# A state-space convolution and a gated MLP on one core: first transform in full matmuls and one-buffer units, statistics on ScalarE, gate products and adds first in the queues

## The chip, the cores and the metric

The kernel runs on one core of one Trainium2 chip. Its time is device microseconds (us) of that core. A profiled execution gives a "span", about 2 us shorter than the run's time. A run is called "slow" when it is over 1.5% above the fastest of the same kernel, and "fast" otherwise. Medians are over all four runs of a kernel; one run each of full2, b_both, dma125 and best1, and one of the kernel before in every set but the second, were slow. All profiles are of fast runs alone. A ratio is the mean time of one kernel's fast runs over that of the other's fast runs of the same rounds, so it is not quite the ratio of the medians quoted.

Engines: PE is TensorE (matmuls), PEld its weight loads, DVE is VectorE, ACT is ScalarE, SP issues the DMAs.

## The reference, cut to what matters

```python
xn = layernorm(A_q)                        # 2048 tokens x 640
# A: causal convolution over all 2048 tokens, per channel, through an FFT of length 4096
kv = (4-tap shift of k) * v
y  = irfft(rfft(kv) * rfft(ssm_k))[:S] + kv * ssm_D
# B: gated MLP, 640 -> 1728 -> 640
h  = sigmoid(xn @ w_gate) * (xn @ w_up)
out = A_q + xn * y + h @ w_down
```

## The kernel before

There are two streams of work. The **MLP** is dense matmuls. The **convolution** is a long chain: ten sub-blocks, each going through tap products (DVE), first transform (PE), eviction (ACT), second transform (PE), eviction (ACT), complex product (DVE), third transform (PE) and eviction (ACT). After five sub-blocks comes a last transform (16 groups of matmuls) for that half of the channels. Its result goes to DRAM, is loaded again in token order, multiplied and added.

A small list scheduler inside the kernel records all operations and fixes the order on every engine from estimated durations, dependences, buffers and priorities (lower number first). PSUM is split into four one-bank buffers `g` (MLP, transposes, last transform) and two two-bank buffers `c` (first three transforms).

```python
def mm2(i, out, lhs, rhs, start, stop):        # two 64-row halves of the array side by side
    for h in range(2):
        rs = slice(64 * h, 64 * h + 64)
        nc.tensor.matmul(out[h], lhsT=lhs[rs], rhs=rhs[rs], start=start, stop=stop)

def rec_st1(idx, pri, dp):                     # first transform of one sub-block: 2 units
    for jq in range(2):
        cs = [f"c1_{idx}_{jq}_{h}" for h in range(2)]     # takes BOTH two-bank buffers
        def f(...):                                       # 8 pairs of 64-row matmuls, 128 columns
            for x in range(2):
                for j in range(4):
                    mm2(j, [q[:, x, j, :] for q in pt], lhs, Fb, True, True)
        pe(8 * mm(128) + 200, f, ..., alloc=[(c, "c") for c in cs] + ...)
        for h in range(2):
            act(1024, <copy c -> T>)
...
def rec_down(tr):                              # down-projection: two g buffers per 128 tokens
    ...
            dve(320, 1, <acc += g>, r=[(pd[i],)], w=[("acc", q)], pri=gpri(pos[0]))
...
# sigmoid (ACT) and gate product (DVE):   pri=pri - BO     with BO = 10
# norm statistics of every block:         8 bn_stats + 4 bn_aggr on DVE for 4 blocks of 128 tokens
```

Of the kernel before, what the change touches and what calls it, by code (L numbers as in the profile page):

```python
# [25 lines left out]
G = 4  # L26
# [15 lines left out]
def _dft_tables():  # L42
    k1 = np.arange(K1, dtype=np.float64)
    n1 = np.arange(N1, dtype=np.float64)
    n2 = np.arange(N2, dtype=np.float64)
    k2 = np.arange(K2, dtype=np.float64)
    odd = 2.0 * k1 + 1.0
    ang = 2.0 * np.pi * np.outer(n1, odd) / 128.0
    F = np.zeros((2, 2, N1, K1, 2, 2))
    for g in range(2):  # L50
        F[:, g, :, :, 0, g] = np.cos(ang)
        F[:, g, :, :, 1, g] = -np.sin(ang)
    F = F.reshape(P, P)
    th = 2.0 * np.pi * n2[:, None, None] * (odd[None, :, None] + 128.0 * k2[None, None, :]) / 8192.0
    M = np.zeros((2, N2, K1, 3, K2))
    M[:, :, :, 0, :] = np.sin(th)[None]
    M[:, :, :, 1, :] = np.cos(th)[None]
    M[:, :, :, 2, :] = -np.sin(th)[None]
    M = M.reshape(P, K1, 3 * K2)
    ph = 2.0 * np.pi * np.outer(k2, n2) / 64.0  # L60
    A = np.zeros((2, K2, N2, 2))
    A[0, :, :, 0] = np.cos(ph)
    A[0, :, :, 1] = np.sin(ph)
    A[1, :, :, 0] = -np.sin(ph)
    A[1, :, :, 1] = np.cos(ph)
    A = A.reshape(P, P)
    t = 64.0 * n1[None, :] + n2[:, None]
    fi = 2.0 * np.pi * odd[:, None, None] * t[None, :, :] / 8192.0
    B = np.zeros((K1, G, N2, 2, G, N1))
    for g in range(G):  # L70
        B[:, g, :, 0, g, :] = np.cos(fi)
        B[:, g, :, 1, g, :] = -np.sin(fi)
    B = B.reshape(P, N2, 2, P)
    J = np.zeros((P, P))
    E = np.zeros((P, P))
    for m in range(P):
        if m % N1:
            J[m - 1, m] = 1.0
        E[m // N1, m] = 1.0
    return _f16_bits(np.concatenate([F, A, J, E], 1)), _f16_bits(M), _f16_bits(B)  # L80
# [164 lines left out]
def kernel(  # L245
# [44 lines left out]
    Mt = cst.tile([P, K1, 3 * K2], U16, name="Mt")  # L290
    Ct = cst.tile([P, 4, P], U16, name="Ct")
    Mb = Mt.bitcast(F16)
    Cb = Ct.bitcast(F16)
    Fb, Ab, Jb, Eb = (Cb[:, i, :] for i in range(4))
    sT = cst.tile([P, 4, CG], BF16, name="sT")
# [9 lines left out]
        "w": ([P, NC, 512], BF16), "xn": ([P, DM], BF16), "xnT": ([P, NC, 512], BF16), "sig": ([P, 512], BF16),  # L305
        "st": ([P, 4, 18], F32), "kt": ([P, 5360], BF16), "vt": ([P, 5120], BF16),
        "ht": ([P, JS, 2, N2], BF16), "kvt": ([P, 2, N2, JS], BF16),
# [13 lines left out]

    def pe(dur, fn, **kw):
        plan.op("PE", dur * 1e-3, fn, **kw)
# [12 lines left out]

    BO = 10.0
    GA, GB = 10.0, 135.0
    CA, CB = 30.0, 210.0

# [33 lines left out]
    def load_small(pri):  # L374
        dma(lambda: nc.sync.dma_start(Ct[:], Cdram.ap().rearrange("p (c n) -> p c n", c=4)), 128, 1024, w=[("C",)], pri=pri)
        dma(lambda: nc.sync.dma_start(tl["sr"].rearrange("p a b -> p (a b)")[0:G], srow.rearrange("o (g n) -> (o g) n", g=G)), 5, 1280, w=[("sr",)], alloc=[("sr", "yt")], pri=pri)
# [98 lines left out]
    def rec_st1(idx, pri, dp):  # L475
        half, sub = divmod(idx, NSUB)
        hb = f"ht{idx}"
        hr = [(hb, g, p) for g in range(G) for p in range(2)]
        T = f"T{idx}"
        for jq in range(2):  # L480
            cs = [f"c1_{idx}_{jq}_{h}" for h in range(2)]

            def f(jq=jq, cs=cs):
                pt = [tl[c].rearrange("p (x j n) -> p x j n", x=2, j=4) for c in cs]
                for x in range(2):
                    for j in range(4):
                        jj = 4 * jq + j
                        lhs = tl[hb][:, jj] if x else tl[f"kvt{idx}"][:, :, :, jj]
                        lhs = lhs.rearrange("p b n -> p (b n)")
                        mm2(j, [q[:, x, j, :] for q in pt], lhs, Fb, True, True)  # L490
            q = pri + dp * jq / 2
            pe(8 * mm(128) + 200, f, r=[("C",), (f"kvt{idx}",)] + hr + ([(T, "a")] if jq else []),
               w=[(c,) for c in cs] + ([] if jq else [(T, "a")]),
               alloc=[(c, "c") for c in cs] + ([] if jq else [(T, "T")]), pri=q)
            for h in range(2):
                act(1024, lambda jq=jq, h=h, c=cs[h]: nc.scalar.copy(
                    out=tl[T][:, jq, :, :, 2 * h:2 * h + 2],
                    in_=tl[c].rearrange("p (x k g) -> p x k g", x=8, g=2)), r=[(cs[h],)], w=[(T, jq, h)], pri=q)

    def rec_st2(idx, pri, dp):  # L500
        T, S_ = f"T{idx}", f"S{idx}"
        for kb in range(2):
            cs = [f"c2_{idx}_{kb}_{b}" for b in range(2)]

            def f(kb=kb, cs=cs):
# [6 lines left out]
            q = pri + dp * kb / 2  # L512
            pe(32 * mm(64) + 250, f, r=[(T, j, h) for j in range(2) for h in range(2)] + ([(S_, "a")] if kb else []) + [("M", kb)],
               w=[(c,) for c in cs] + ([] if kb else [(S_, "a")]),
# [29 lines left out]
    def rec_st3(idx, pri, dp):  # L544
        half, sub = divmod(idx, NSUB)
        S_ = f"S{idx}"
        for b in range(2):
            c = f"c3_{idx}_{b}"

            def f(b=b, c=c):  # L550
                pa = tl[c].rearrange("p (q j n) -> p q j n", q=2, j=4)
                for q in range(2):
                    for j in range(4):
                        nc.tensor.matmul(pa[:, q, j, :], lhsT=tl[S_][:, 4 * b + 2 * q, j * P:(j + 1) * P], rhs=Ab,
                                         start=True, stop=True)

            def ev(b=b, c=c):
                d0 = 16 * sub + 8 * b
                nc.scalar.copy(out=vview(half).rearrange("p n r d -> p (n r) d")[:, :, d0:d0 + 8],
                               in_=tl[c].rearrange("p (j n) -> p n j", j=8))  # L560
            q = pri + dp * b / 2
            z = sub == 0 and b == 0
            pe(8 * mm(128), f, r=[(S_, "R", 0), (S_, "R", 1), ("C",)], w=[(c,)],
               alloc=[(c, "c")] + ([("V", "V")] if idx == 0 and b == 0 else []), pri=q)
            act(1024, ev, r=[(c,)], w=[("V", (sub + 1 - half) % 6, b)], pri=q)

    def rec_st4(half, pri, dp):
        vr_ = [("V", s + 1 - half, b) for s in range(NSUB) for b in range(2)]
        for q in range(8):
            y = f"yt{half}_{q}"  # L570
            for e in range(2):
# [13 lines left out]
                pq = pri + dp * i4 / 16  # L585
                pe(8 * mm(80), f, r=[(bt,)] + vr_, w=[(c,)], alloc=[(c, "g")], pri=pq)
                act(320, lambda y=y, c=c, e=e: nc.scalar.activation(
# [8 lines left out]
    def rec_ln(tr, pri, spri):  # L596
# [13 lines left out]
        vi = lambda: tl[b].bitcast(I32)[:, :, 15]  # L610
        for i in range(4):
            for s2 in range(2):
# [7 lines left out]
        def rsq():  # L620
            nc.vector.tensor_scalar(ve(), var(), 1e-5, None, op0=ALU.add)
            nc.vector.tensor_scalar(yi(), vi(), 1, None, op0=ALU.logical_shift_right)
# [13 lines left out]
        for i in range(4):  # L636
# [3 lines left out]
            dve(640, 2.2, lambda i=i, x_=x_: nc.vector.tensor_scalar(  # L640
                tl[x_][:], acc[:, 4 * tr + i, :], mv(i)[:, 0:1], tl[b][:, i, 14:15], op0=ALU.subtract, op1=ALU.mult),
                r=[("acc", 4 * tr + i), (b, i, "r"), (b, i, "mv")], w=[(x_,)], alloc=[(x_, "xn")],
# [11 lines left out]
    def rec_fc(tr, n):  # L654
# [5 lines left out]
        for u in range(1 if last else 2):  # L660
# [21 lines left out]
            if last:  # L682
                act(512, lambda c=c: nc.scalar.activation(tl[sg][64:P, :], tl[c][0:64, :], ACT.Sigmoid),
                    r=[(c,)], w=[(sg,)], alloc=[(sg, "sig")], pri=pri - BO)
                dve(512, 1, lambda c=c: nc.vector.tensor_tensor(hT[64:P, fc, :], tl[sg][64:P, :], tl[c][64:P, :],
                                                                ALU.mult),
                    r=[(c,), (sg,)], w=[(hk, fc)], pri=pri - BO)
            elif u == 0:
                act(512, lambda c=c: nc.scalar.activation(tl[sg][:], tl[c][:], ACT.Sigmoid),
                    r=[(c,)], w=[(sg,)], alloc=[(sg, "sig")], pri=pri - BO)  # L690
            else:
                dve(512, 1, lambda c=c: nc.vector.tensor_tensor(hT[:, fc, :], tl[sg][:], tl[c][:], ALU.mult),  # L692
                    r=[(c,), (sg,)], w=[(hk, fc)], pri=pri - BO)

    def rec_down(tr):
        hT = hTs[tr % 2]
        hk = f"hT{tr % 2}"
        for t4 in range(4):
# [18 lines left out]
            for i in range(2):  # L717
                dve(320, 1, lambda i=i, q=q, pd=pd: nc.vector.tensor_tensor(
                    acc[:, q, 320 * i:320 * i + 320], tl[pd[i]][:, 0:320], acc[:, q, 320 * i:320 * i + 320], ALU.add),
                    r=[(pd[i],)], w=[("acc", q)], pri=gpri(pos[0]))  # L720

# [3 lines left out]
    def rec_xhat(pri):  # L725
# [6 lines left out]
        for q in range(NQ):  # L732
            st = f"st{q // 4}"
            dve(640, 2.2, lambda q=q, st=st: nc.vector.tensor_scalar(
                xqv(q), xqv(q), tl[st][:, q % 4, 12:13], tl[st][:, q % 4, 14:15], op0=ALU.subtract, op1=ALU.mult),
                r=[(st, q % 4, "r"), (st, q % 4, "mv")], w=[(f"xq{q // 8}", q)], pri=pri - 3)
# [151 lines left out]
```

## Time and profile before

| | us |
|---|---|
| median run (timed with the changed kernel) | 285.7 |
| span of the profile | 281.4 |
| PE busy / PE idle | 255.8 / 25.6 |
| DVE busy, ACT busy | 206.3, 154.6 |

The page of the kernel before: engine totals, then PE's busy tenths and granted clock (tenths of full speed) in 40 equal slices.

```profile
span 281.4 us, 7503 instructions
...
PE 255.8 (91%) x3176; PEld 157.4 (56%) x3176; DVE 206.3 (73%) x356; ACT 154.6 (55%) x215; POOL 0.7 (0%) x6
...
PE   7989999998997946999999897999999999999980
...
PEclk9999999999999975999999998999999999999996
```

PE is the fullest engine. The two low clock digits (7 and 5) are at 98 to 113 us. The windows view of the same kernel gives length, busy time and count per engine, then granted clock, DMA share and GB/s:

```profile
80.00:120.00 40.00, 31.53 (x515) 23.69 (x513) 38.19 (x65) 27.31 (x34) 0.00 (x0) 0.87 0.59 69
220.00:260.00 40.00, 38.76 (x413) 25.51 (x412) 23.55 (x43) 16.49 (x30) 0.00 (x0) 1.00 0.61 159
260.00:281.40 21.40, 13.60 (x101) 9.58 (x98) 10.07 (x24) 0.00 (x0) 0.00 (x0) 0.87 0.76 192
```

There are two holes: 8.5 us of PE idle from 80 to 120 us at a lowered clock, and the end. The timeline view shows the first hole's cause. Columns are start, length, engine, line, operation, output and inputs, and in brackets the idle time before it and what ended it.

```profile
97.37 0.30 PE L705 MATMUL g_1436<-wd,hT_80 128*128 128x320 bf16 x1
...
108.55 0.48 DVE L718 TENSOR_TENSOR acc<-g_1317,acc 128x320 bf16<-128x320 f32 x1
...
109.08 0.69 PE L646 MATMUL g_1713<-ident,xn_1529 128*128 128x128 bf16 x5 [2.10 <-DVE acc L718]
...
111.04 0.48 DVE L718 TENSOR_TENSOR acc<-g_1318,acc 128x320 bf16<-128x320 f32 x1
...
112.61 0.48 DVE L718 TENSOR_TENSOR acc<-g_1435,acc 128x320 bf16<-128x320 f32 x1
```

The granted clock (third number from the end) was 0.50 from 101.8 to 112.0 us:

```profile
101.80:112.04 10.24, 6.96 (x155) 6.26 (x155) 9.62 (x13) 6.11 (x8) 0.00 (x0) 0.50 0.18 27
```

PE finished the first two down-projection results (`g_1317`, `g_1318`) at about 92.7 us and the next two at 97.7. DVE began to add them 15 to 18 us later. All four `g` buffers were held until then, so no MLP matmul could run.

### The profile page before, as it was taken

Reading aid. Unit: us, or ns where it says so; the run is one execution under the profiler, and the core shown is the slowest. Engines: PE = TensorE matmul, PEld = TensorE weight load, DVE = VectorE, ACT = ScalarE, POOL = GpSimd, SP = SyncE. Lnnn points to the kernel's source line nnn. Section 1 sums busy time; section 2 is a strip of 40 time slices with the busy share of each in tenths; the row PEclk is TensorE's granted clock in tenths of the full one; section 3 lists DMA queues with packets and bytes.
Section 4 is the critical chain, followed back from the end, with each engine's and each line's share of the span. In section 5 each row is a group of like instructions: output and inputs, shape, how many; then the busy total and the mean of one; then the engine's idle time right before and its main releaser. Section 6 shows DMA issues by size and latency. Waiting matters only on the chain.

```text
span 281.4 us, 7503 instructions
## 1 busy us (share of the span) xinstructions
PE 255.8 (91%) x3176; PEld 157.4 (56%) x3176; DVE 206.3 (73%) x356; ACT 154.6 (55%) x215; POOL 0.7 (0%) x6
## 2 busy tenths in 40 slices
PE   7989999998997946999999897999999999999980
PEld 2844344554545746776775655555545555677760
DVE  7862998899999998998949783057197899412382
ACT  2652324666585485975558876677667646222000
POOL 0000000000000000000000000000000000000000
PEclk9999999999999975999999998999999999999996
DMA  7999886976397920071231576541449357754687
GB/s 203 268 150 146 211 272 141 350 190 168 50 153 104 141 31 13 12 190 45 40 95 21 152 204 227 172 132 48 159 123 341 78 95 182 210 185 170 113 199 273
DMA packets 106993, 42.62 MB, mean 151 GB/s; under 512 B 77196, under 2 KB 102608, under 8 KB 106960
## 3 DMA queue, kind: packets, MB, share of 16 engines
q1 hardware_dynamic: 106960, 42.14, 64.5%
q8 instruction: 25, 0.41, 0.6%
q14 instruction: 8, 0.07, 0.1%
HBM read 36.89 MB, written 5.24 MB: 150 GB/s over the span
## 4 chain that ended last, share of the span: by engine, by line
PE 43%; DMA 9%; DVE 7%; issue 2%; SPq 1%; ACT 0%; DVEq 0%; ACTq 0%
DMA B_2908<-dftB 2%; DMA B_4171<-dftB 2%; DMA B_2729<-dftB 2%; DMA yd<-yt_4298 2%; SPq L437 1%; DMA ht_1899<-in_A_ssm_k_dram 1%; PE g_4389 L705 1%; PE g_2142 L705 1%; PE g_2202 L705 1%; PE g_2288 L705 1%; PE g_2398 L705 1%; PE g_4516 L705 1%; PE g_4471 L705 1%; PE g_4431 L705 1%; PE g_4470 L705 1%
## 5 line engine op out<-in xcount | busy, mean ns | idle before, releaser
L705 PEld LDWEIGHTS <-hT_81 128*128 128x128 bf16 x224 | 21.4, 98 | 9.0 <-issue 0.7
L473 PEld LDWEIGHTS <-Mt 64*128 64x128 f16 x1280 | 21.8, 97 | 7.9 <-issue 7.6
L705 PEld LDWEIGHTS <-hT_80 128*128 128x128 bf16 x224 | 21.0, 98 | 8.7 <-issue 1.1
L779 PE MATMUL c_88<-sig_85,ident 128*128 128x512 bf16 x26 | 8.4, 477 | 1.7 <-POOL ident masks.py:199 1.4
L666 PEld LDWEIGHTS <-w_435 128*128 128x128 bf16 x40 | 3.8, 98 | 5.8 <-DMA w_435<-in_B_w_gate_dram 0.9
L666 PEld LDWEIGHTS <-w_806 128*128 128x128 bf16 x40 | 3.7, 98 | 5.2 <-DMA w_806<-in_B_w_gate_dram 1.0
L666 PEld LDWEIGHTS <-w_562 128*128 128x128 bf16 x40 | 3.8, 98 | 4.4
L666 PEld LDWEIGHTS <-w_2301 128*128 128x128 bf16 x40 | 3.8, 104 | 4.4 <-issue 1.1
L666 PEld LDWEIGHTS <-w_487 128*128 128x128 bf16 x40 | 3.8, 98 | 4.4
L666 PEld LDWEIGHTS <-w_3610 128*128 128x128 bf16 x40 | 3.8, 98 | 4.3
L779 PEld LDWEIGHTS <-ident 128*128 128x128 bf16 x26 | 2.8, 116 | 5.8 <-issue 3.3
L666 PEld LDWEIGHTS <-w_121 128*128 128x128 bf16 x40 | 3.8, 98 | 4.0
L666 PEld LDWEIGHTS <-w_2876 128*128 128x128 bf16 x40 | 3.7, 98 | 4.2
L666 PEld LDWEIGHTS <-w_3171 128*128 128x128 bf16 x40 | 3.7, 98 | 4.1
L666 PEld LDWEIGHTS <-w_3371 128*128 128x128 bf16 x40 | 3.6, 98 | 4.0
L692 DVE TENSOR_TENSOR hT_80<-sig_3039,g_3022 128x512 bf16<-128x512 bf16 x1 | 0.7, 689 | 7.0 <-PE g_3022 L666 7.0
L666 PEld LDWEIGHTS <-w_2067 128*128 128x128 bf16 x40 | 3.6, 98 | 3.8
L666 PEld LDWEIGHTS <-w_932 128*128 128x128 bf16 x30 | 2.8, 97 | 3.4 <-issue 0.4
L676 PEld LDWEIGHTS <-w_98 128*128 128x128 bf16 x80 | 4.6, 98 | 0.0
L613 DVE BATCH_NORM_STATS2 st_105<-acc 128x6 f32<-128x320 bf16 x8 | 3.6, 467 | 1.2 <-DMA acc<-in_A_q_dram 1.2
L531 DVE TENSOR_TENSOR Sb_3277<-S_3053 64x2048 bf16<-64x2048 bf16 x2 | 2.4, 1220 | 2.7 <-ACT S_3053 L517 2.7
L666 PEld LDWEIGHTS <-w_3814 128*128 128x128 bf16 x30 | 2.8, 98 | 2.8
(867 smaller groups left out, 805.0 us busy)
## 6 DMA issues: line engine op xcount, KB each, us to landing
out_dram<-acc SPq DMA_DIRECT2D x8, 320.0 KB, 3.5
acc<-in_A_q_dram SPq DMA_DIRECT2D x3, 640.0 KB, 6.6
Mt<-dftM SPq DMA_DIRECT2D x2, 768.0 KB, 6.3
wd<-in_B_w_down_dram SPq DMA_DIRECT2D x3, 480.0 KB, 4.8
kt_139<-in_A_k_dram SPq DMA_DIRECT2D x4, 320.0 KB, 7.4
vt_190<-in_A_v_dram SPq DMA_DIRECT2D x4, 320.0 KB, 7.1
kt_1114<-in_A_k_dram SPq DMA_DIRECT2D x4, 320.0 KB, 8.2
vt_1329<-in_A_v_dram SPq DMA_DIRECT2D x4, 320.0 KB, 7.6
```

The lines of the kernel that those rows point to most:

```text
L437: dma(lambda g=g, p=p, c0=c0: nc.sync.dma_start(tl[b][g * N1:(g + 1) * N1, :, p, :], h3[:, c0:c0 + JS, :]), 5.5 * JS, 128, w=[(b, g, p)], ...
L473: nc.tensor.matmul(out[h], lhsT=lhs[rs], rhs=rhs[rs], start=start, stop=stop)
L531: dve(2 * JS * P, 2, lambda o=hv[h], i=hv[1 - h]: nc.vector.tensor_tensor(tl[Sb][o], xh(0)[o], xh(1)[i], ALU.mult), r=sk, w=[(Sb, h)], all ...
L613: dve(320, 1, lambda i=i, s2=s2: nc.vector.bn_stats(stat(i, s2), acc[:, 4 * tr + i, s2 * 320:(s2 + 1) * 320]), r=[("acc", 4 * tr + i)], w= ...
L666: nc.tensor.matmul(tl[c][:], lhsT=tl[wb][:, k, o:o + P], rhs=tl[X][:, k, :], start=(k == 0), stop=(k == NC - 1))
L676: nc.tensor.matmul(tl[c][:, ts], lhsT=tl[wb][:, k, o:o + P], rhs=tl[X][:, k, ts], start=(k == 0), stop=(k == NC - 1))
L692: dve(512, 1, lambda c=c: nc.vector.tensor_tensor(hT[:, fc, :], tl[sg][:], tl[c][:], ALU.mult), r=[(c,), (sg,)], w=[(hk, fc)], pri=pri - BO)
L705: nc.tensor.matmul(tl[pd[i]][:, 0:320], lhsT=hT[:, fc, t4 * P:(t4 + 1) * P], rhs=wd[:, fc, 320 * i:320 * i + 320], start=(fc == 0), stop=( ...
L779: plan.op("PE", 0.43 if i < 13 else 0.22, lambda: nc.tensor.matmul(tl["wps"][:, 0:512], lhsT=ident[:], rhs=tl["warm"][:], start=True, stop ...
```

## The change

The intent: evict the first transform one buffer at a time, with each matmul filling the whole array; take work off DVE in its full stretch; and free PSUM sooner by placing gate products and adds ahead of everything else on ACT and DVE. Two further edits come with it: convolution matmuls first on PE (`FST`), and four numbers (`GA, GB, CA, CB`) that spread the convolution among the MLP work.

```diff
-    F = np.zeros((2, 2, N1, K1, 2, 2))          # table 128 x 128, two channel groups per half
+    F = np.zeros((G, N1, K1, 2, G))             # table 128 x 256, four groups at once
 def rec_st1:
-        for jq in range(2):
-            cs = [f"c1_{idx}_{jq}_{h}" for h in range(2)]
-                        mm2(j, [q[:, x, j, :] for q in pt], lhs, Fb, True, True)
-            pe(8 * mm(128) + 200, f, ..., alloc=[(c, "c") for c in cs] + ...)
+        for u in range(4):
+            jq, x = divmod(u, 2)
+            c = f"c1_{idx}_{u}"                  # ONE two-bank buffer
+                    nc.tensor.matmul(pt[:, j, :], lhsT=..., rhs=Fb, start=True, stop=True)   # x4
+            pe(4 * mm(256), f, first=FST, ..., alloc=[(c, "c")] + ...)
 ... (first=FST on the other transforms too; FST = 1000.0, subtracted from the priority)
 def rec_ln:
+        for i in range(4 if tr >= 2 else 0):     # blocks 8 to 15: two ACT passes each
+            Copy(scale=-1/640, accum_out=-mean); Square(bias=-mean, accum_out=sum)
-        for i in range(4):
+        for i in range(4 if tr < 2 else 0):      # bn_stats on DVE
 sigmoids and gate products:
-                    pri=pri - BO
+                    pri=-1.0
 down-projection adds:
-                    pri=gpri(pos[0])
+                    pri=-1.0
-    GA, GB = 10.0, 135.0
-    CA, CB = 30.0, 210.0
+    GA, GB = 20.0, 140.0
+    CA, CB = 35.0, 200.0
```

More of the change, by code (lines that the diff above doesn't have):

```diff
@@ L48, in _dft_tables @@
     ang = 2.0 * np.pi * np.outer(n1, odd) / 128.0
-    F = np.zeros((2, 2, N1, K1, 2, 2))
-    for g in range(2):
-        F[:, g, :, :, 0, g] = np.cos(ang)
-        F[:, g, :, :, 1, g] = -np.sin(ang)
-    F = F.reshape(P, P)
+    F = np.zeros((G, N1, K1, 2, G))
+    for g in range(G):
+        F[g, :, :, 0, g] = np.cos(ang)
+        F[g, :, :, 1, g] = -np.sin(ang)
+    F = F.reshape(P, 2 * P)
     th = 2.0 * np.pi * n2[:, None, None] * (odd[None, :, None] + 128.0 * k2[None, None, :]) / 8192.0
@@ L290 @@
     Mt = cst.tile([P, K1, 3 * K2], U16, name="Mt")
-    Ct = cst.tile([P, 4, P], U16, name="Ct")
+    Ct = cst.tile([P, 5 * P], U16, name="Ct")
     Mb = Mt.bitcast(F16)
     Cb = Ct.bitcast(F16)
-    Fb, Ab, Jb, Eb = (Cb[:, i, :] for i in range(4))
+    Fb, Ab, Jb, Eb = Cb[:, 0:2 * P], Cb[:, 2 * P:3 * P], Cb[:, 3 * P:4 * P], Cb[:, 4 * P:5 * P]
     sT = cst.tile([P, 4, CG], BF16, name="sT")
@@ L305 @@
         "w": ([P, NC, 512], BF16), "xn": ([P, DM], BF16), "xnT": ([P, NC, 512], BF16), "sig": ([P, 512], BF16),
-        "st": ([P, 4, 18], F32), "kt": ([P, 5360], BF16), "vt": ([P, 5120], BF16),
+        "st": ([P, 4, 17], F32), "kt": ([P, 5360], BF16), "vt": ([P, 5120], BF16),
         "ht": ([P, JS, 2, N2], BF16), "kvt": ([P, 2, N2, JS], BF16),
@@ L320, in make, with pe @@
         return pool.tile(shape, dt, name=f"{tag}{i}", tag=f"{tag}{i}")
-    def pe(dur, fn, **kw):
+    FST = 1000.0
+    def pe(dur, fn, first=0.0, **kw):
+        kw["pri"] -= first
         plan.op("PE", dur * 1e-3, fn, **kw)
@@ L335, in mm @@
         return n / 2.4 + 3.0
-    BO = 10.0
-    GA, GB = 10.0, 135.0
-    CA, CB = 30.0, 210.0
+    GA, GB = 20.0, 140.0
+    CA, CB = 35.0, 200.0
     def gpri(p):
@@ L374, in load_small @@
     def load_small(pri):
-        dma(lambda: nc.sync.dma_start(Ct[:], Cdram.ap().rearrange("p (c n) -> p c n", c=4)), 128, 1024, w=[("C",)], pri=pri)
+        dma(lambda: nc.sync.dma_start(Ct[:], Cdram.ap()), 160, 1280, w=[("C",)], pri=pri)
         dma(lambda: nc.sync.dma_start(tl["sr"].rearrange("p a b -> p (a b)")[0:G], srow.rearrange("o (g n) -> (o g) n", g=G)), 5, 1280, w=[("sr",)], alloc=[("sr", "yt")], pri=pri)
@@ L479, in rec_st1, with f @@
         T = f"T{idx}"
-        for jq in range(2):
-            cs = [f"c1_{idx}_{jq}_{h}" for h in range(2)]
-            def f(jq=jq, cs=cs):
-                pt = [tl[c].rearrange("p (x j n) -> p x j n", x=2, j=4) for c in cs]
-                for x in range(2):
-                    for j in range(4):
-                        jj = 4 * jq + j
-                        lhs = tl[hb][:, jj] if x else tl[f"kvt{idx}"][:, :, :, jj]
-                        lhs = lhs.rearrange("p b n -> p (b n)")
-                        mm2(j, [q[:, x, j, :] for q in pt], lhs, Fb, True, True)
-            q = pri + dp * jq / 2
-            pe(8 * mm(128) + 200, f, r=[("C",), (f"kvt{idx}",)] + hr + ([(T, "a")] if jq else []),
-               w=[(c,) for c in cs] + ([] if jq else [(T, "a")]),
-               alloc=[(c, "c") for c in cs] + ([] if jq else [(T, "T")]), pri=q)
-            for h in range(2):
-                act(1024, lambda jq=jq, h=h, c=cs[h]: nc.scalar.copy(
-                    out=tl[T][:, jq, :, :, 2 * h:2 * h + 2],
-                    in_=tl[c].rearrange("p (x k g) -> p x k g", x=8, g=2)), r=[(cs[h],)], w=[(T, jq, h)], pri=q)
+        for u in range(4):
+            jq, x = divmod(u, 2)
+            c = f"c1_{idx}_{u}"
+            def f(jq=jq, x=x, c=c):
+                pt = tl[c].rearrange("p (j n) -> p j n", j=4)
+                for j in range(4):
+                    jj = 4 * jq + j
+                    lhs = tl[hb][:, jj] if x else tl[f"kvt{idx}"][:, :, :, jj]
+                    nc.tensor.matmul(pt[:, j, :], lhsT=lhs.rearrange("p b n -> p (b n)"), rhs=Fb, start=True, stop=True)
+            q = pri + dp * u / 4
+            pe(4 * mm(256), f, first=FST, r=[("C",)] + (hr if x else [(f"kvt{idx}",)]) + ([(T, "a")] if u else []),
+               w=[(c,)] + ([] if u else [(T, "a")]), alloc=[(c, "c")] + ([] if u else [(T, "T")]), pri=q)
+            act(1024, lambda jq=jq, x=x, c=c: nc.scalar.copy(
+                out=tl[T][:, jq, 4 * x:4 * x + 4].rearrange("p j k g -> p (j k g)"), in_=tl[c][:]),
+                r=[(c,)], w=[(T, u)], pri=q)
     def rec_st2(idx, pri, dp):
@@ L512, in rec_st2 @@
             q = pri + dp * kb / 2
-            pe(32 * mm(64) + 250, f, r=[(T, j, h) for j in range(2) for h in range(2)] + ([(S_, "a")] if kb else []) + [("M", kb)],
+            pe(32 * mm(64) + 250, f, first=FST, r=[(T, u) for u in range(4)] + ([(S_, "a")] if kb else []) + [("M", kb)],
                w=[(c,) for c in cs] + ([] if kb else [(S_, "a")]),
@@ L562, in rec_st3 @@
             z = sub == 0 and b == 0
-            pe(8 * mm(128), f, r=[(S_, "R", 0), (S_, "R", 1), ("C",)], w=[(c,)],
+            pe(8 * mm(128), f, first=FST, r=[(S_, "R", 0), (S_, "R", 1), ("C",)], w=[(c,)],
                alloc=[(c, "c")] + ([("V", "V")] if idx == 0 and b == 0 else []), pri=q)
@@ L585, in rec_st4 @@
                 pq = pri + dp * i4 / 16
-                pe(8 * mm(80), f, r=[(bt,)] + vr_, w=[(c,)], alloc=[(c, "g")], pri=pq)
+                pe(8 * mm(80), f, first=FST, r=[(bt,)] + vr_, w=[(c,)], alloc=[(c, "g")], pri=pq)
                 act(320, lambda y=y, c=c, e=e: nc.scalar.activation(
@@ L610, in rec_ln, with f1, f2 @@
         vi = lambda: tl[b].bitcast(I32)[:, :, 15]
-        for i in range(4):
+        for i in range(4 if tr >= 2 else 0):
+            x_ = f"xs{tr}_{i}"
+            ac = ("acc", 4 * tr + i)
+            def f1(i=i, x_=x_):
+                nc.scalar.activation(tl[x_][:], acc[:, 4 * tr + i, :], ACT.Copy, scale=-1.0 / DM, accum_out=tl[b][:, i, 12:13])
+            def f2(i=i, x_=x_):
+                nc.scalar.activation(tl[x_][:], acc[:, 4 * tr + i, :], ACT.Square, bias=tl[b][:, i, 12:13],
+                                     accum_out=tl[b][:, i, 13:14])
+            act(640, f1, r=[ac], w=[(x_,), (b, i, "nm")], alloc=[(x_, "xn")] + ([(b, "st")] if i == 0 else []), pri=spri)
+            act(640, f2, r=[ac, (b, i, "nm")], w=[(x_,), (b, i, "mv")], pri=spri)
+        for i in range(4 if tr < 2 else 0):
             for s2 in range(2):
@@ L620, in rsq @@
         def rsq():
-            nc.vector.tensor_scalar(ve(), var(), 1e-5, None, op0=ALU.add)
+            nc.vector.tensor_scalar(ve(), var(), 1.0 / DM if tr >= 2 else 1.0, 1e-5, op0=ALU.mult, op1=ALU.add)
             nc.vector.tensor_scalar(yi(), vi(), 1, None, op0=ALU.logical_shift_right)
@@ L640, in rec_ln @@
             dve(640, 2.2, lambda i=i, x_=x_: nc.vector.tensor_scalar(
-                tl[x_][:], acc[:, 4 * tr + i, :], mv(i)[:, 0:1], tl[b][:, i, 14:15], op0=ALU.subtract, op1=ALU.mult),
+                tl[x_][:], acc[:, 4 * tr + i, :], mv(i)[:, 0:1], tl[b][:, i, 14:15],
+                op0=ALU.add if tr >= 2 else ALU.subtract, op1=ALU.mult),
                 r=[("acc", 4 * tr + i), (b, i, "r"), (b, i, "mv")], w=[(x_,)], alloc=[(x_, "xn")],
@@ L683, in rec_fc @@
                 act(512, lambda c=c: nc.scalar.activation(tl[sg][64:P, :], tl[c][0:64, :], ACT.Sigmoid),
-                    r=[(c,)], w=[(sg,)], alloc=[(sg, "sig")], pri=pri - BO)
+                    r=[(c,)], w=[(sg,)], alloc=[(sg, "sig")], pri=-1.0)
                 dve(512, 1, lambda c=c: nc.vector.tensor_tensor(hT[64:P, fc, :], tl[sg][64:P, :], tl[c][64:P, :],
                                                                 ALU.mult),
-                    r=[(c,), (sg,)], w=[(hk, fc)], pri=pri - BO)
+                    r=[(c,), (sg,)], w=[(hk, fc)], pri=-1.0)
             elif u == 0:
                 act(512, lambda c=c: nc.scalar.activation(tl[sg][:], tl[c][:], ACT.Sigmoid),
-                    r=[(c,)], w=[(sg,)], alloc=[(sg, "sig")], pri=pri - BO)
+                    r=[(c,)], w=[(sg,)], alloc=[(sg, "sig")], pri=-1.0)
             else:
                 dve(512, 1, lambda c=c: nc.vector.tensor_tensor(hT[:, fc, :], tl[sg][:], tl[c][:], ALU.mult),
-                    r=[(c,), (sg,)], w=[(hk, fc)], pri=pri - BO)
+                    r=[(c,), (sg,)], w=[(hk, fc)], pri=-1.0)
     def rec_down(tr):
@@ L719, in rec_down @@
                     acc[:, q, 320 * i:320 * i + 320], tl[pd[i]][:, 0:320], acc[:, q, 320 * i:320 * i + 320], ALU.add),
-                    r=[(pd[i],)], w=[("acc", q)], pri=gpri(pos[0]))
+                    r=[(pd[i],)], w=[("acc", q)], pri=-1.0)
     def xqv(q):
@@ L734, in rec_xhat @@
             dve(640, 2.2, lambda q=q, st=st: nc.vector.tensor_scalar(
-                xqv(q), xqv(q), tl[st][:, q % 4, 12:13], tl[st][:, q % 4, 14:15], op0=ALU.subtract, op1=ALU.mult),
+                xqv(q), xqv(q), tl[st][:, q % 4, 12:13], tl[st][:, q % 4, 14:15],
+                op0=ALU.add if q >= 8 else ALU.subtract, op1=ALU.mult),
                 r=[(st, q % 4, "r"), (st, q % 4, "mv")], w=[(f"xq{q // 8}", q)], pri=pri - 3)
```

## The prediction

> **What bounds it now.** TensorE: the page gives PE 255.8 of 281.4 us busy, DVE 206.3, ACT 154.6. By windows, though, DVE is the second limit from 40 to 140 us: 93.4 of 100 us busy. In 80-100 and 100-120 us it is busy 16.64 and 14.89 of 20, at a granted clock of 0.74 in the second.
>
> The timeline shows why. The first down-projection groups end on PE at about 92.5 us, but their adds into acc (g_1317, g_1318, g_1435, g_1436) run on DVE only at 108.55-113.4 us, behind norm statistics, taps and products. They hold all four one-bank PSUM buffers ("g"), so no filler matmul can start. Waits of PE between 97 and 114 us: 1.15, 0.70, 1.09, 0.18, 0.70, 2.10, 0.66, together 6.6 us. The idle also halves the clock (skill, "TensorE: Matmul & The Clock Gate", on re-throttling; here matmuls of the second transform take 238 ns instead of 188, and the slices show 7 and 5). My estimate of the clock's cost, from blocks that take 2.7 and 1.9 us instead of 1.0, is 4 us. The stall costs about 11 us.
>
> **What changes.**
> - Adds and gate products first on DVE: buffers come free about 0.5-2 us after PE ends. Removes most of the 11 us, and the wait of 1.58 us at 88 us.
> - Statistics of blocks 8-15: 16 bn_stats (0.46 us) and 8 aggregates (0.19) leave DVE, about 8-9 us of the saturated stretch. ACT gains 16 passes over 640 columns, about 0.7 us each (as the 128x640 copies), 11 us; ACT was busy 60-75% there, so it fits.
> - First transform: a pair-packed unit of 16 half matmuls costs 0.62 us from its start to the next matmul (chain: 187.64 to 188.26), against 8 x 54 ns streaming. The rest is mode switch (skill, "TensorEngine Tiling (Array Packing)", Key Properties: changing mode drains TensorE; this trace agrees). Full matmuls of 256 columns: 8 x 109 ns (half of the 512-column spacing, 216 ns) = 0.87 us. So PE pays 0.25 x 20 = **5 us more**. In return eviction (1.01 us) and matmul can alternate.
> - Tail: after the last down matmul, DVE now does two adds and one final add instead of six operations: about -1 us.
>
> **Sum, on the critical path.** 281.4 + 5 (PE work) - 10 (stall and clock) - 2 (gate-product waits and DVE-late spots) - 1 (tail) = 273.4 us of span; runs read about 2 us longer. The waits for the last transform's tables at 158-173 us (2.5 us idle, clock 0.91) stay: same three buffers and queue. Predicted **275 us**, 268.5 to 282; faster 0.80, same 0.17, slower 0.03.
>
> **What would show each step.**
> - PE stays at about 252-256 us busy (5 more work, 4 less clock), its share rises to 93% or more.
> - No slice between 80 and 125 us below 9 for PE; clock 1.0 there; adds into acc within 2 us of their matmuls.
> - First-transform matmuls 256 columns, about 109 ns apart, 160 of them; 0.87 us per two units.
> - DVE about 198 us, ACT about 165 us.
> - No PE wait over 1 us on adds or gate products; table waits remain.
>
> **What would make it wrong.** ACT's statistics passes in front of evictions of the first and second transform, so that conv-first matmuls wait at PE's head. The conv's chain (evict, product, taps) still too slow, so that filler runs out elsewhere. Worse collisions of table loads with weight loads. Then 280-285. If the freed DVE removes nearly all idle before 225 us, 268.

(In its first paragraph the 16.64 and 14.89 of 20 us are PE's busy time, not DVE's.)

## More of the kernel before

The cost of a paired first-transform unit can be read from the timeline too. Five MLP matmuls take 1.08 us from start to start (65.83 to 66.91):

```profile
66.91 1.24 PE L666 MATMUL g_953<-xnT_131,w_806 128*128 128x512 bf16 x5
68.08 0.28 PE L473 MATMUL c_973<-Ct,kvt_550 64*128 64x128 f16 x1
...
68.70 0.61 PE L666 MATMUL g_954<-xnT_131,w_806 128*128 128x512 bf16 x2
```

From 66.91 + 1.08 = 67.99 to 68.70 is 0.71 us for eight pairs, of which about 0.45 is streaming (0.056 us a pair).

Chips differ between sets of runs, and each set carries its own runs of the kernel before.

## The result, and the profile after

The changed kernel takes 272.6 us (272.1 to 272.9, four runs) against 285.7 us. The ratio is 0.958, interval 0.949 to 0.966. That is 13.1 us by the medians and 10.6 us by the spans (the profile of the kernel before is of a 283.3 us run).

The page of the changed kernel:

```profile
span 270.8 us, 7185 instructions
...
PE 254.7 (94%) x3016; PEld 160.1 (59%) x3016; DVE 199.4 (74%) x332; ACT 166.2 (61%) x247; POOL 0.7 (0%) x6
...
PE   7989799989989899999999989999999999999993
...
PEclk9999999999999999999999999999999999999998
```

Its windows:

```profile
80.00:120.00 40.00, 38.11 (x581) 27.53 (x580) 35.68 (x57) 35.76 (x53) 0.00 (x0) 1.00 0.67 103
220.00:260.00 40.00, 39.20 (x355) 26.41 (x353) 19.13 (x43) 10.02 (x22) 0.00 (x0) 1.00 0.73 188
260.00:270.80 10.80, 6.09 (x45) 4.16 (x43) 2.88 (x7) 0.00 (x0) 0.00 (x0) 0.90 0.45 157
```

PE's busy time is nearly the same (255.8 to 254.7). What fell is its idle time, 25.6 to 16.1 us: 6.6 us of that between 80 and 120 us, and 3.1 us in the tail after the last matmul (273.6 to 281.4 before, 266.1 to 270.8 now). Busy time alone hides part of this, since the same matmuls are also busy for longer at a lowered clock.

The first two adds now start 0.3 and 1.7 us after their last matmul (timeline of the changed kernel):

```profile
95.44 0.30 PE L717 MATMUL g_1191<-wd,hT_80 128*128 128x320 bf16 x1
...
95.88 0.49 DVE L730 TENSOR_TENSOR acc<-g_1190,acc 128x320 bf16<-128x320 f32 x1
...
97.42 0.48 DVE L730 TENSOR_TENSOR acc<-g_1191,acc 128x320 bf16<-128x320 f32 x1
```

The other adds of the first half (1024 tokens) wait up to 3.5 us.

Two of the new first-transform units, with the MLP matmul that follows:

```profile
61.54 0.60 PE L491 MATMUL c_851<-Ct,kvt_555 128*128 128x256 f16 x4
...
61.98 0.60 PE L491 MATMUL c_859<-Ct,ht_507 128*128 128x256 f16 x4
...
62.42 1.24 PE L678 MATMUL g_865<-xnT_131,w_753 128*128 128x512 bf16 x5
```

Two units take 0.88 us where one paired unit of the same work took 0.71. The change makes PE do 20 x 0.17 = 3.4 us more, not less.

A new cost shows at 20 to 60 us, where PE is busy 36.9 us instead of 39.4: it waits for loads (the first line below). From the waits of PE in the changed kernel (waited for: total, times, longest):

```profile
PE g_425 L424 <- DMA kt_140<-in_A_k_dram: 1.6, 1, 1.6
...
PE c_1433 L491 <- ACT T_1411 L495: 1.1, 1, 1.1
PE g_2704 L581 <- DMA B_2608<-dftB: 0.9, 1, 0.9
```

### The profile page after: what moved, and what is told of

It reads as the page before. It is cut to its first block, busy times and chain, and to the rows that moved or that the text cites. A ratio compares the mean times of both kernels' runs of the same rounds, so it can differ in the third digit from the quotient of the medians.

```text
span 270.8 us, 7185 instructions
## 1 busy us (share of the span) xinstructions
PE 254.7 (94%) x3016; PEld 160.1 (59%) x3016; DVE 199.4 (74%) x332; ACT 166.2 (61%) x247; POOL 0.7 (0%) x6
## 4 chain that ended last, share of the span: by engine, by line
PE 53%; SPq 14%; DVE 11%; DMA 11%; ACT 5%; issue 3%; DVEq 0%; ACTq 0%
SPq L439 4%; SPq L421 4%; SPq L419 3%; DMA w_627<-in_B_w_up_dram 3%; DMA yd<-yt_2751 2%; DMA B_4087<-dftB 2%; DMA B_3848<-dftB 1%; DVE acc L730 1%; DMA B_2608<-dftB 1%; DMA w_436<-in_B_w_gate_dram 1%; ACT S_924 L516 1%; DMA w_1787<-in_B_w_gate_dram 1%; DVE Sb_1765 L530 1%; DVE t_1727 L461 1%; PE g_2117 L717 1%
## 5 line engine op out<-in xcount | busy, mean ns | idle before, releaser
L717 PEld LDWEIGHTS <-hT_80 128*128 128x128 bf16 x224 | 21.2, 98 | 7.6
L475 PEld LDWEIGHTS <-Mt 64*128 64x128 f16 x1280 | 20.2, 93 | 6.8 <-issue 6.5
L530 DVE TENSOR_TENSOR Sb_3405<-S_3218 64x2048 bf16<-64x2048 bf16 x2 | 2.4, 1222 | 2.3 <-ACT S_3218 L516 2.2
L530 DVE TENSOR_TENSOR Sb_1425<-S_1244 64x2048 bf16<-64x2048 bf16 x2 | 2.4, 1221 | 2.2 <-ACT S_1244 L516 2.1
```

Source lines behind the costliest of these rows:

```text
L530: dve(2 * JS * P, 2, lambda o=hv[h], i=hv[1 - h]: nc.vector.tensor_tensor(tl[Sb][o], xh(0)[o], xh(1)[i], ALU.mult), r=sk, w=[(Sb, h)], all ...
L717: nc.tensor.matmul(tl[pd[i]][:, 0:320], lhsT=hT[:, fc, t4 * P:(t4 + 1) * P], rhs=wd[:, fc, 320 * i:320 * i + 320], start=(fc == 0), stop=( ...
```

## The experiments

Theory A, that of the prediction: the late adds were the main loss, so the queue places are the main gain, and the first transform costs PE time for little return. Rivals: B, the first transform's one-buffer units are the gain; C, the statistics leaving DVE are the gain. From the second set on there is a Theory D, formed from the first set.

For each run, the table also gives three readings: PE busy between 80 and 120 us with the granted clock; the mean period of the convolution's sub-blocks (start of the second transform of the tenth minus that of the first, over 9); and the end of the last transform's last matmul group ("conv end"), with what is left of the span after it. The last matmul groups of the last transform in the kernel before and in the changed one:

```profile
259.02 0.45 PE L582 MATMUL g_4399<-V_1294,B_4360 128*128 128x80 bf16 x8
243.90 0.45 PE L581 MATMUL g_4175<-V_1180,B_4127 128*128 128x80 bf16 x8
```

| kernel | median us | ratio to before | PE busy 80-120, clock | period | conv end | span minus conv end |
|---|---|---|---|---|---|---|
| before | 284.3 to 285.7 by set | 1 | 31.5, 0.87 | 18.0 | 259.5 | 21.9 |
| changed | 272.6 | 0.958 | 38.1, 1.00 | 16.4 | 244.4 | 26.4 |
| u_adds | 277.4 | 0.975 | 34.5, 1.00 | 16.2 | 242.9 | 32.9 |
| u_st1 | 291.0 | 1.022 | 37.8, 1.00 | 18.2 | 265.7 | 22.6 |
| u_stats | 272.0 | 0.955 | 37.9, 0.96 | 16.3 | 241.8 | 26.4 |
| u_gates | 279.6 | 0.985 | 36.0, 0.96 | 16.5 | 245.2 | 32.1 |
| pairs1 | 272.3 | 0.954 | 37.8, 0.96 | 16.5 | 244.7 | 26.4 |
| full2 | 294.2 | 1.034 | 37.1, 1.00 | 18.8 | 270.3 | 21.2 |
| b_queue | 291.4 | 1.021 | 37.6, 1.00 | 18.3 | 265.8 | 23.5 |
| b_units | 284.3 | 0.996 | 31.7, 0.91 | 17.1 | 251.0 | 31.6 |
| b_both | 273.8 | 0.963 | 35.1, 1.00 | 16.0 | 241.8 | 29.1 |
| u_knots | 280.8 | 0.988 | 34.5, 0.96 | 16.0 | 245.4 | 34.0 |
| dma125 | 274.1 | 0.963 | 39.1, 1.00 | 16.8 | 247.5 | 22.6 |
| best1 | 271.8 | 0.957 | 38.6, 1.00 | 16.7 | 245.2 | 22.6 |

All gave correct results; each has four runs, timed over three rounds.

### First set: one part undone at a time

**u_adds**, the adds back to their late place:

```diff
-   r=[(pd[i],)], w=[("acc", q)], pri=-1.0)
+   r=[(pd[i],)], w=[("acc", q)], pri=gpri(pos[0]))
```

> The changed kernel with one thing undone: the adds of the down-projection go back to their late place in the VectorE queue. Theory A (the gain is the early release of the four one-bank buffers by the adds): the stall near 100-115 us comes back, adds start more than 5 us after their matmuls, the clock falls there, 279 us or more. Theory B (the gain is the first transform's single two-bank units): 273 to 275 us. Theory C (the gain is the statistics leaving VectorE): 273 to 275 us.

277.4 us, so 4.8 us of the gain needs this line. PE is idle for 5.5 of the 40 us from 80 to 120, 3.6 more than in the changed kernel. The clock stayed at 1.00, so the stall is only partly back. That is less than A asked for, and more than B and C.

**u_st1**, the whole first transform as before, with the old table; `first=FST` kept:

```diff
-   for u in range(4):   4 x matmul(256 columns),   alloc=[(c, "c")]
+   for jq in range(2):  8 x mm2(pair, 128 columns), alloc=[(c, "c") for c in cs], first=FST
```

> The changed kernel with the first transform put back to pairs of half matmuls that take both two-bank buffers (everything else kept). Theory B: the waits for both buffers come back, 280 us or more. Theory A: PE work falls by 5 us (0.25 x 20 units), busy PE near 250 us, and the time falls or stays, 268 to 273 us. Theory C: as A.

291.0 us: slower than the kernel before. A had expected 268 to 273, so A falls. PE busy did fall (250.9 us), as A had it, but the time rose by 18 us. The early hole is still filled; the loss is at the end. Windows of u_st1, then its longest wait of PE:

```profile
220.00:260.00 40.00, 31.52 (x411) 23.03 (x411) 18.73 (x33) 14.69 (x23) 0.00 (x0) 0.91 0.51 128
260.00:288.30 28.30, 12.25 (x114) 8.91 (x112) 9.93 (x24) 1.64 (x4) 0.00 (x0) 0.80 0.66 175
```

```profile
PE g L584 <- DVE acc L733: 6.6, 1, 6.6
```

That wait is not where the convolution falls behind: the third transform of its tenth sub-block, before the wait, already ends at 236.2 us, against 217.9 in the changed kernel.

**u_stats**, statistics of all blocks on DVE again:

```diff
-   for i in range(4 if tr >= 2 else 0):   # ACT passes
-   for i in range(4 if tr < 2 else 0):    # bn_stats
+   for i in range(4):                     # bn_stats
```

> The changed kernel with the statistics of blocks 8 to 15 back on VectorE as bn_stats. VectorE gains about 8 us and ScalarE loses about 12. Theory C (the gain is mostly this relief): 279 us or more. Theory A: VectorE is full only from 100 to 140 us (39 of 40), so part of the 8 us shows, 274 to 277 us.

272.0 us (270.0 to 273.1), not to be told from the changed kernel. C falls, and so does A's 274 to 277. DVE is 6.4 us busier, ACT 11.1 us less, and the time does not care.

**u_gates**, sigmoids and gate products back to their old priority:

```diff
-   pri=-1.0        # sigmoid, gate product
+   pri=pri - 10.0
```

> The changed kernel with the sigmoids and gate products back at their old priority (ten below that of their matmul). Every theory: a little slower, 273 to 276 us, since the buffers of gate and up matmuls come free later behind taps and products; if gate products were the main part of the gain, 279 us or more.

279.6 us, slower by 7.0. That is above the 273 to 276 of every theory and inside the branch "279 us or more": next to the rest of the change, the places of the gate products are worth more than those of the adds (4.8).

B had u_st1 right and u_adds wrong. After this set, **Theory D**: the program has two ends, and both must be early. PE must not run out of buffers (late adds and gate products), and the convolution's chain must end early enough. After its last transform there are still the store, the loads, products and adds: 22.6 us in u_st1 (and 21 to 24 in full2 and b_queue below), of which PE has work for only the first few. Freeing the MLP's buffers alone lets the MLP run ahead of the convolution. One-buffer units shorten the chain.

The traces of the three slowest kernels agree. Their last gate or up matmul ends at 220.5 (b_queue), 222.2 (full2) and 223.6 us (u_st1), 13 to 18 us before the third transform of the tenth sub-block does (235.8, 240.4, 236.2). In the changed kernel it ends at 233.0, 15 us after that transform (217.9), so the MLP still has work to fill in.

### Second set: the form and the buffering apart, and each part alone

**pairs1**, one-buffer units kept, in the same order on every engine, but with paired half matmuls:

```diff
-   for j in range(4): nc.tensor.matmul(pt[:, j, :], lhsT=lhs, rhs=Fb)        # 256 columns
+   for j in range(4): mm2(j, [q[:, j, :] for q in pt], lhs, Fb, True, True)  # one half per bank
```

> The changed kernel with the same units of one two-bank buffer each and the same order on every engine, but the matmuls of a unit are again pairs of 64-row halves (one half per bank). Theory D (what the first transform's change is worth is the unit of one buffer, which shortens the convolution's chain; the form of the matmul is not): within 1 us of the changed kernel's 272.6 us, since a unit of four pairs should cost 4 x 55 ns plus about 0.2 us of mode switch, 0.42 us, against 0.44 us for four full matmuls. Rival E (the full matmul itself is the gain, by doing away with the mode switches): 278 us or more.

272.3 us, as D had it. With one-buffer units the form of the matmul costs and brings nothing: in its timeline, a unit of four pairs takes 0.43 us from the end of the MLP matmuls before it (179.37 + 1.08 = 180.45) to the next one (180.88), and a full unit takes 0.44.

```profile
179.37 1.25 PE L680 MATMUL g<-xnT,w 128*128 128x512 bf16 x5
180.55 0.40 PE L475 MATMUL c<-Ct,ht 64*128 64x128 f16 x8
180.88 1.25 PE L680 MATMUL g<-xnT,w 128*128 128x512 bf16 x5
```

**full2**, full matmuls but two buffers per unit:

```diff
-   for u in range(4):   alloc=[(c, "c")]
+   for jq in range(2):  alloc=[(c, "c") for c in cs]     # 8 full matmuls, then two evictions
```

> The changed kernel with the full 256-column matmuls, but in units that take both two-bank buffers at once as before. Theory D: as slow as the kernel with the whole first transform undone (291.0 us) or slower by up to 5 us, since PE has 5 us more to do: 289 to 296 us, with the convolution's last matmul near 265 us. Rival E: 273 to 276 us.

294.2 us (one run, 297.7, was slow), and the conv end is 270.3 where D said "near 265". So the unit of one buffer, with the order that the scheduler plans from it, is the whole value of this part. Against u_st1 (291.0, of another set), which differs by the form of the matmul, full matmuls cost 3.2 us by the medians and 1.3% by the ratios, close to the 3.4 us read above.

**b_queue**, the kernel before with only the queue places:

```diff
-   pri=pri - BO            # sigmoid, gate product
-   pri=gpri(pos[0])        # down-projection adds
+   pri=-1.0                # all three
```

> The kernel before with only the queue places of the change: sigmoids, gate products and down-projection adds first. Theory A as predicted (this is the main gain, 10 to 12 us): 273 to 277 us. Theory D: the stall at 97-114 us goes, but the convolution's chain is as long as before, so the other matmuls run out ahead of it and PE starves at the end: 283 to 292 us, with idle after 220 us in place of that at 100 us.

291.4 us: 5.9 us *slower* than before (ratio 1.021, interval 1.014 to 1.028). This is the prediction's main gain on its own. The early hole is gone (37.6 of 40 busy, clock 1.00), and everything is lost at the end. Windows of b_queue, then its longest waits of PE:

```profile
220.00:260.00 40.00, 30.03 (x402) 22.17 (x400) 21.89 (x43) 14.29 (x23) 0.00 (x0) 0.87 0.51 128
260.00:289.30 29.30, 12.34 (x115) 8.97 (x112) 10.02 (x24) 1.64 (x4) 0.00 (x0) 0.79 0.63 168
```

```profile
PE g L582 <- DVE acc L718: 6.4, 1, 6.4
PE c L554 <- DVE S L537: 3.5, 1, 3.5
```

Its last down-projection matmul ends at 272.3 us, 17 us before the span does. The convolution ends at 265.8, 6.3 us later than before. Part of that is there before the last transform: the third transform of the tenth sub-block ends at 235.8, against 232.2. That gate products and adds now go ahead of the convolution's own work on DVE would explain this part; it was not isolated. The rest comes with the 6.4 us wait. This wait, at 236 to 242 us, is a last-transform group that waits for a `g` buffer: four down results stand in them until 241.6 us, while DVE works through final products and adds that stood ahead of theirs. A wait of 6.6 us at this place is in u_st1 and full2 too, and in neither the kernel before nor the changed one. No run takes it away, so how slow b_queue would be without it is open.

**b_units**, the kernel before with only the new first transform (and its table):

```diff
-   for jq in range(2):  8 x mm2(pair, 128 columns), alloc=[(c, "c") for c in cs]
+   for u in range(4):   4 x matmul(256 columns),   alloc=[(c, "c")]
```

> The kernel before with only the first transform of the change: full matmuls, units of one two-bank buffer. Theory A: late adds still hold the one-bank buffers, 284 to 290 us. Theory D: the chain shortens (last matmul of the last transform before 250 us instead of 259), the stall near 100 us stays, 276 to 283 us.

284.3 us, not to be told from the kernel before (ratio 0.996, interval 0.990 to 1.002). The convolution ends 8.5 us earlier, yet the early hole is as deep as before (31.7 of 40):

```profile
80.00:120.00 40.00, 31.72 (x555) 22.07 (x553) 38.59 (x79) 28.28 (x34) 0.00 (x0) 0.91 0.56 76
```

D had the direction of the parts right, though the conv end of 251.0 just misses its "before 250". Its time (276 to 283) was too low; that PE had 3.4 us more to do may be why, but this is argued, not shown.

### Third set: both parts, the numbers, and tries at more

**b_both**, the diffs of b_units and b_queue together on the kernel before:

> The kernel before with two parts of the change together: the first transform in full matmuls and units of one two-bank buffer, and sigmoids, gate products and adds first. Alone they gave 284.3 and 291.4 us. Theory D (each part only uncovers the other's limit: late adds at 100 us, or a convolution that ends last): most of the gain at once, 272 to 277 us. If the two were independent, the sum of their effects: about 290 us.

273.8 us (fast runs 272.7 to 274.3; one more, 277.4, was slow). Alone the two parts gave -1.3 and +5.9 us; together they give -10.5. So the gain needs both at once. That each part removes what the other part's gain runs into is the reading that fits the traces: the hole of b_units is partly filled, and the idle end of b_queue is gone. Windows of b_both:

```profile
80.00:120.00 40.00, 35.09 (x607) 24.77 (x605) 38.71 (x82) 27.65 (x34) 0.00 (x0) 1.00 0.55 70
220.00:260.00 40.00, 38.74 (x331) 25.66 (x330) 21.94 (x48) 9.03 (x19) 0.00 (x0) 1.00 0.81 213
```

Statistics, `FST` and the new numbers are not in this kernel. What they add (272.6 to 273.8) is within the scatter.

**u_knots**, the changed kernel with the old four numbers:

```diff
-   GA, GB = 20.0, 140.0;  CA, CB = 35.0, 200.0
+   GA, GB = 10.0, 135.0;  CA, CB = 30.0, 210.0
```

> The changed kernel with the four numbers that spread the convolution among the other matmuls back at their old values. Theory D: the convolution is given less time at first and more at the end, so filler and convolution are less well matched, 275 to 281 us; if the numbers do not matter, 272 to 274 us.

280.8 us. The numbers matter by 8 us here, though b_both, which has the old ones too, loses nothing. The conv end is 245.4, not later than in the changed kernel, so D's reason (worse matched at the end) is not what happened. The loss is PE idle at 80 to 160 us (72.1 of 80 us busy against 77.0). Which of the remaining parts the numbers answer to is left open.

**dma125**, the scheduler told that loads of short rows take 14% longer:

```diff
-   kb * 1.1 / run if run < 512
+   kb * 1.25 / run if run < 512
```

> The changed kernel, planned with loads of short rows 14% longer (the eight loads of k and v took 2.4 us each in its trace, the plan had 2.2), so that their readers stand later in the TensorE queue. Theory D (PE work is now the bound and what is left over is waits for late loads, 3.1 us of idle from 20 to 60 us): 270 to 272.5 us, the wait of the halo matmul of 1.6 us gone.

274.1 us (fast runs 272.0 to 275.0; one more, 276.2, was slow): a miss. The wait on loads did shrink (74.3 of the first 80 us busy against 72.9), and between 120 and 220 us the new order lost 2.9 us (95.5 busy against 98.4).

**best1**, no statistics on ACT, the longer loads, `GA, GB = 25, 140`, `CA, CB = 35, 190`, and the priorities of the later norm blocks at 75 and 80:

> The changed kernel without the statistics on ScalarE, planned with the longer loads, and with slightly different numbers for the spread. A try at a faster version: 268 to 272 us if theory D is right that the statistics do nothing for the time.

271.8 us (its fast runs 269.6 to 273.1; one more, 275.7, was slow). Not to be told from the changed kernel. No version here clearly beats it.

## Why the prediction was right, point by point

The time (275 predicted, 272.6 measured) and the direction were right. Much of the reasoning was not, and that the time came so close was luck.

- **The early stall, right.** PE busy 80-120 us went from 31.5 to 38.1, the clock from 0.87 to 1.00, and the first adds came within 1.7 us of their matmuls. The Trainium skill's "TensorE: Matmul & The Clock Gate", Part 1: The HAM clock gate, says that an idle window lets the clock fall back to half. The trace agrees: where the idle went, the clock of 0.50 from 101.8 to 112.0 us went. Here the idle came in pieces, though: no single wait of PE in the 20 us before 101.8 was longer than 1.6 us.
- **"Adds and gate products first on DVE ... Removes most of the 11 us", as a saving of time on its own: wrong.** It does remove the stall (b_queue), and the kernel gets 5.9 us slower. The failed step is "Sum, on the critical path", which took the stall off the span without asking what ends last. The kernel before was already close to its other end: 21.9 us from conv end to span end, within the range of the three kernels where PE is left waiting for the convolution (21.2 to 23.5). Its timeline shows both ends together: DVE still waits for loads of the convolution's result 2 us before it waits for the last down-projection result. In the changed kernel the last product with such a load starts at 259.7 us, 6.3 us before the last down-projection matmul ends.

```profile
271.46 0.89 DVE L756 TENSOR_TENSOR S_4482<-S_4482,vt_3642 128x640 bf16<-128x640 bf16 x2 [0.66 <-DMA S_4482<-yd]
273.50 0.49 DVE L718 TENSOR_TENSOR acc<-g_4516,acc 128x320 bf16<-128x320 f32 x1 [0.35 <-PE g_4516 L705]
```

- **Gate products as a small term: under-sized.** They shared -2 us of the sum with "DVE-late spots"; undoing their places alone costs 7.0 us next to the rest of the change (u_gates).
- **The first transform as a cost with little return: wrong.** The cost was 3.2 to 3.4 us, not 5: the prediction took 0.62 us for a paired unit and left out its lead-in of 0.09. The return was left out of the sum. With the queue places in, undoing this part costs 18 us (u_st1), through the buffering alone (pairs1, full2).
- **Statistics, half right.** DVE fell by 6.9 us (8 to 9 predicted). ACT rose by 11.6 (11 predicted), though a pass takes more than the 0.7 us estimated, see below. The time did not move (u_stats). No separate term had been given for it, but the "saturated stretch" was offered as a gain.
- **The tail, under-sized.** -1 us predicted; it went from 7.8 to 4.7 us, because the convolution now ends 22 us before the last matmul and only adds are left.
- **Table waits "stay": mostly wrong.** PE at 160-180 us went from 17.5 of 20 busy at a clock of 0.91 to 19.5 at 1.00; table waits in PE's list fell from 3.5 to 1.8 us. No run isolates why.
- **Not foreseen:** 2.5 us of new waits for loads at 20-60 us.

The two wrong terms nearly cancelled: the credit given to the queue places (10 + 2 us) is about what the *pair* of parts brings (10.5).

What stays open: how one-buffer units shorten a sub-block. The period fell from 18.0 to 16.4 us. From a second transform's start to the next first transform it went from 8.2 to 7.4 us on average, and from there to the next second transform from 9.7 to 9.0: a little everywhere, as it would if units start as soon as *one* buffer is free. That is an inference; no run isolates it. `FST` was not tested alone. Every edit also makes the scheduler plan another order; only pairs1 keeps the order and changes one thing.

## What to carry to other kernels

Before crediting a removed stall, find what ends last and how much slack it has. Here a dense filler and a long dependent chain share the engines, and speeding the filler alone made the program slower. An operation that claims two buffers at once must wait for both; halving the claim was worth 18 us here, once the queue places were in, even though it made the matmul engine's own work longer; without them it was worth nothing that could be measured. When two parts of a change each look useless or harmful alone, run the four combinations before dropping either.

## What the Trainium skill lacked or had wrong

- "TensorEngine Tiling (Array Packing)", Key Properties, says that changing the tiling mode drains TensorE, but not what that costs. Here eight pairs of 64-row, 128-column matmuls between full-array matmuls take 0.71 us against about 0.45 of streaming, so about 0.26 us in and out; four pairs take 0.43, no less than four full 256-column matmuls (0.44). So the eight pairs gained 0.17 us over the full matmuls of the same work, the four pairs nothing.
- "ScalarE: Activation LUTs" says that an ACTIVATE can give an accumulator output, but not that this is a second instruction with its own time: 0.19 to 0.24 us for each of the 16 passes, on top of 0.72 to 0.88 us for 128x640 bf16. In the trace of the changed kernel:

```profile
68.79 0.73 ACT L615 ACTIVATE xn_990<-acc 128x640 bf16<-128x640 bf16 x1
69.42 0.20 ACT L615 ACTIVATION_READ_ACCUMULATOR xn_990<-acc 128x1 f32 x1
```

- "Perfetto Trace Analysis", Identifying the Most-Contended Engine, says to optimize the engine with the highest occupancy first (for TensorE it judges the headroom by weight-load busy time and matmul rate instead). Here u_st1 shows the limit of that: it has the lowest PE busy time of all these kernels (250.9 us), and a lower PEld busy time than the changed one (154.0 to 160.1), and is 18 us slower. The section has no step that asks which chain ends last and how much slack the others have (a later one, "Optimization Strategies", does speak of engines that block the critical path).
